# Loading the first slices of x in a gated GELU kernel: halves on two queues, and DMA transposes for slices 5 to 7

## The chip, the core and the metric

The kernel runs on one core of a Trainium2 chip. The metric is the time of one execution on the device in microseconds (us). Three executions of the kernel before took 592.37, 591.83 and 591.96 us; their median is 591.96 us. One more execution was profiled, and all rows shown below are from it.

## What is computed

x has 2048 rows of 1024, w_gate and w_up are 1024 by 3584, w_down is 3584 by 1024; everything is bfloat16.

```
g = jnp.einsum("bsd,df->bsf", x, w_gate)
u = jnp.einsum("bsd,df->bsf", x, w_up)
h = _gelu(g) * u            # tanh form
return jnp.einsum("bsf,fd->bsd", h, w_down)
```

## The kernel before, in words

The 2048 rows go in two halves of 1024, and each half in two chunks of 512 rows (`SCH`). TensorE needs x with the 1024 columns on the partitions, so a chunk is kept transposed as eight tiles `xT[c][ko]`, 128 by 512 each. "Slice ko" below means the 128 columns of x (or the 128 rows of a weight) that belong to `ko`. The 3584 hidden columns are 28 blocks of 128 in eight groups of 3, 3, 3, 3, 4, 4, 4, 4. For each block and chunk, eight matmuls 128x512 (one for each slice, L103) give g and eight give u. ScalarE and VectorE make `hT` of them (class `Evac`, L113 to L139). After all eight groups of a half, L307 multiplies `hT` by `w_down`, and the result is stored.

The schedule is written by hand (`manual_schedule`, L168): each engine runs its instructions in the order of the code.

**How the kernel begins.** Nothing is in the chip's memory yet, and the first group (three blocks, first chunk) is computed in an order of its own, `first_group` (L251): for slice 0, then slice 1 and so on, six matmuls, three with w_gate and three with w_up, into six PSUM banks. So slice k of x, of w_gate and of w_up must be there when step ko=k starts, and each step is 6 matmuls.

Meanwhile TensorE runs `dummy` matmuls (L174) on a constant: six before the first transposes (L182), then one of 512 and one of 256 columns behind them (L255, L256).

Of the first chunk of x, slices 0 to 5 (`NTURN = 6`) are loaded as they lie (`xpart`, L185, into the tiles `xn`) and turned on TensorE (`turn`, L224): four 128x128 transposes into a PSUM bank (L231), which VectorE copies to `xT` (L237; for slice 0 in two halves, L240 and L241). `turn(0)` stands ahead of everything, `turn(1)` behind the fifth matmul of step ko=0, and each other `turn(ko + 1)` behind the second matmul of step ko. Slices 6 and 7 are DMA transposes (`xload`, L96), which need no work on TensorE.

The loads go out from two queues, SP (`S`) and ACT (`A`), in the order of L200 to L217: x slice 0 on SP and w_gate slice 0 on ACT first, then the others, and the two DMA transposes last on SP. On ACT, a load of the Sigmoid table (L180) and a Square of one column (L181, which reads `gate`, set by VectorE at L178) stand ahead of the DMAs. Behind the first group's loads SP issues the weights of groups 1 and 2 (L219, L220, 768 KB each) and eight DMA transposes for the second chunk (L222).

**Waits between DMAs.** The framework hands eight completion counters round over the DMAs of both queues, in the program's merged order. A DMA on a counter that is in use waits, on its queue, until the DMA eight places earlier has landed; everything behind it on that queue waits too. In the kernel before, x slices 2-3 and w_gate slice 2 go out without a wait. w_up slice 2 waits for x slice 0, w_gate slice 3 for w_gate slice 1, w_gate slices 4-5 for x slices 2-3, w_gate slices 6-7 for w_gate slice 2, the first DMA transpose for w_up slice 2, the second for x slices 4-5.

Of the kernel before, what the change touches and what calls it, by code (L numbers as in the profile page):

```python
# [14 lines left out]
def kernel(  # L15
# [11 lines left out]
    nc = tc.nc  # L27
    P = nc.NUM_PARTITIONS
    bf16 = mybir.dt.bfloat16
    f32 = mybir.dt.float32  # L30
    ACT = mybir.ActivationFunctionType
    ALU = mybir.AluOpType

    x2 = x.flatten_outer_dims()
    out2 = out.flatten_outer_dims()
    S, Dm = x2.shape
    Df = w_gate.shape[1]
    NKB = Dm // P
    NFB = Df // P
    SCH = 512  # L40
# [6 lines left out]
    GROUPS = [3, 3, 3, 3, 4, 4, 4, 4]  # L47
# [5 lines left out]
    NST = 4  # L53
    WDF = 4
    NWARM = 6
    NTURN = 6
    TPC = SCH // P

    pool = ctx.enter_context(tc.tile_pool(name="sb", bufs=1))
# [11 lines left out]
    st_ring = [pool.tile([P, DMW], bf16, name=f"st{r}") for r in range(NST)]  # L71
    warm = nc.const_aps.tensor(1.0, (P, SCH), bf16)
    ident = pool.tile([P, P], bf16, name="ident")
    xn = [pool.tile([P, TPC, 2 * P], bf16, name=f"xn{q}") for q in range(NTURN // 2)]
    banks = [psum.tile([P, 512], f32, name=f"bank{b}") for b in range(8)]

    nbank = 0
# [1 line left out]
    def bank():  # L79
        nonlocal nbank  # L80
        b = banks[nbank % 8]
        nbank += 1
        return b
# [12 lines left out]
    def xload(half, c, ko):  # L96
        s0 = half * HS + c * SCH
        nc.sync.dma_start_transpose(
            out=xT[c][ko], in_=x2[s0 : s0 + SCH, ko * P : (ko + 1) * P]
        )  # L100

    def mm1(ps, w, j, c, ko):
        nc.tensor.matmul(  # L103
            ps,
            lhsT=w[:, ko, j * P : (j + 1) * P],
            rhs=xT[c][ko],
            start=(ko == 0),
            stop=(ko == NKB - 1),
        )
# [57 lines left out]

    ctx.enter_context(tc.manual_schedule())  # L168

    gate = pool.tile([P, SCH], bf16, name="gate")  # L170
    gated = pool.tile([P, 1], f32, name="gated")

    def dummy(b, n=SCH):
        nc.tensor.matmul(b[:, :n], lhsT=warm[:, :P], rhs=warm[:, :n], start=True, stop=True)  # L174

    nc.vector.memset(gate, 0.0)  # L178
    make_identity(nc, ident)
    nc.scalar.preload_act_table(ACT.Sigmoid)  # L180
    nc.scalar.activation(gated, gate[:, :1], ACT.Square)  # L181
    for _ in range(NWARM):  # L182
        dummy(banks[5])

    def xpart(eng, ko, n):  # L185
        eng.dma_start(
            out=xn[ko // 2][:, :, (ko % 2) * P : (ko % 2 + n) * P],
            in_=x2[0:SCH, ko * P : (ko + n) * P].rearrange("(t p) d -> p t d", p=P),
        )

    def wpart(eng, ring, w, ko, n):
        eng.dma_start(
            out=ring[0][:, ko : ko + n, : GROUPS[0] * P],
            in_=w[ko * P : (ko + n) * P, : GROUPS[0] * P].rearrange("(ko ki) f -> ki ko f", ki=P),
        )


    S, A = nc.sync, nc.scalar
    G, U = (wg_ring, w_gate), (wu_ring, w_up)
    xpart(S, 0, 1)  # L200
    wpart(A, *G, 0, 1)
    wpart(S, *U, 0, 1)
    xpart(A, 1, 1)
    wpart(S, *G, 1, 1)
    wpart(A, *U, 1, 1)
    xpart(S, 2, 2)
    xpart(A, 4, 2)
    wpart(S, *G, 2, 1)
    wpart(S, *U, 2, 1)
    wpart(S, *G, 3, 1)  # L210
    wpart(A, *U, 3, 1)
    wpart(S, *G, 4, 2)
    wpart(A, *U, 4, 2)
    wpart(S, *G, 6, 2)
    wpart(A, *U, 6, 2)
    for ko in range(NTURN, NKB):
        xload(0, 0, ko)  # L217
    for n in (1, 2):
        wload(nc.sync, wg_ring, w_gate, n, n)  # L219
        wload(nc.sync, wu_ring, w_up, n, n)  # L220
# [3 lines left out]
    def turn(ko):  # L224


        tp = [banks[6 + ko % 2].bitcast(bf16)] * 2
        if ko == 0:
            tp = [banks[6].bitcast(bf16), banks[7].bitcast(bf16)]
        for t in range(TPC):  # L230
            nc.tensor.transpose(  # L231
                tp[t // (TPC // 2)][:, t * P : (t + 1) * P],
                xn[ko // 2][:, t, (ko % 2) * P : (ko % 2 + 1) * P],
                ident,
            )
        if ko:
            nc.vector.tensor_copy(out=xT[0][ko], in_=tp[0][:, :SCH])  # L237
        else:
            h = SCH // 2
            nc.vector.tensor_copy(out=xT[0][ko][:, :h], in_=tp[0][:, :h])  # L240
            nc.vector.tensor_copy(out=xT[0][ko][:, h:], in_=tp[1][:, h:SCH])  # L241
# [9 lines left out]
    def first_group():  # L251
        wg, wu = wg_ring[0], wu_ring[0]
        ps = [(bank(), bank()) for _ in range(GROUPS[0])]
        turn(0)
        dummy(banks[5])  # L255
        dummy(banks[5], SCH // 2)  # L256
        n0 = GROUPS[0]
        for ko in range(NKB):
            steps = [(b, j) for j in range(n0) for b in range(2)]
            if ko == 0:  # L260
                steps = [(b, j) for b in range(2) for j in range(n0)]
            for i, (b, j) in enumerate(steps):
                mm1(ps[j][b], (wg, wu)[b], j, 0, ko)
                if i == (4 if ko == 0 else 1) and ko + 1 < NTURN:
                    turn(ko + 1)
        e = [Evac(ps[j][0], ps[j][1], j, 0) for j in range(GROUPS[0])]
        e[0].square()
        e[1].square()
        e[0].cubic()
        e[0].sigmoid()  # L270
        e[1].cubic()
        e[2].square()
        e[0].gelu()
        e[0].product()
        e[1].sigmoid()
        e[2].cubic()
        e[1].gelu()
        e[1].product()
        e[2].sigmoid()
        e[2].gelu()  # L280
        e[2].product()
# [34 lines left out]
    for half in range(NHALF):  # L316
        base = half * NG
        if half == 0:
            first_group()
            group(1, [0], ahead=2)  # L320
            group(2, [0])
            for g in range(NG):
                group(g, [1] if g < NW else range(HSC))
                i = g - 1
                if 0 <= i < len(wd):
                    for q in range(i, len(wd) if g == NG - 1 else i + 1):
                        nc.sync.dma_start(
                            out=wd[q],
                            in_=w_down[q * WDF * P : (q + 1) * WDF * P, :].rearrange(
                                "(fo fi) d -> fi fo d", fi=P  # L330
                            ),
                        )
                prefetch(g + 3)
        else:
            for g in range(NG):
                group(base + g, range(HSC))
                prefetch(base + g + 3)
        k = 0
        xnext = [(c, ko) for c in range(HSC) for ko in range(NKB)] if half + 1 < NHALF else []
        for ss in range(HS // P):  # L340
            for dc in range(NDC):
# [8 lines left out]
                if xnext:  # L350
                    c, ko = xnext.pop(0)
# [31 lines left out]
```

## Time and profile before

| what | us |
|---|---|
| median of three executions | 591.96 |
| profiled execution, its own time | 591.85 |
| span of its profile, first to last instruction | 590.1 |
| around the span (591.85 - 590.1) | 1.75 |
| TensorE busy | 583.5 (99%) |
| dummies (L174), eight, busy | 3.6 |
| transposes on TensorE (L231), 24, busy | 2.6 |
| DMA transposes (L98), 26, median from issue to landing | 2.7 |

A row of the timeline reads: start in us from the beginning of the span, us, engine, line, operation, output<-input, shape, xcount, and in brackets the idle time before it with what ended it. SPq and ACTq rows are the issuing of a DMA by that queue. PEld is TensorE's weight load, PE its matmul. The us of a matmul is from its start to its modelled end; matmuls overlap, so what a matmul costs in a stream is read from one start to the next start. A row of the DMA view gives out<-in, the issuing queue, xcount, the size, and the us from issue to landing. A row of the chain of waits gives start, us, and the work that the end of the program waited for.

### The profile page before, as it was taken

How to read it: one execution, taken by the hardware profiler on the slowest of the kernel's cores; microseconds unless marked ns; L12 is line 12 of the kernel's file. 1: busy time of each engine (PE TensorE's matmuls, PEld its weight loads, DVE VectorE, ACT ScalarE, POOL GpSimd, SP SyncE). 2: the span in 40 equal slices, each digit the busy share in tenths (PEclk: the TensorE clock that was granted, in tenths of full speed). 3: DMA queues.
4: the chain of work that ended last, by engine and by line, in shares of the span. 5: the costliest groups of instructions: out<-in, count | busy, mean ns of one | idle time of the engine just before them, and what ended most of it. 6: DMA issues, size and time to landing. Idle time of an engine off the chain costs nothing.

```text
span 590.1 us, 6588 instructions
## 1 busy us (share of the span) xinstructions
PE 583.5 (99%) x2723; PEld 269.1 (46%) x2776; DVE 244.0 (41%) x361; ACT 147.7 (25%) x243; POOL 0.7 (0%) x6
## 2 busy tenths in 40 slices
PE   9999999999999999999999999999999999999998
PEld 4444444444444444444444444444444444444445
DVE  1765665565656400000046565566556562000000
ACT  1443333333333200000023333333333331000000
POOL 0000000000000000000000000000000000000000
PEclk9999999999999999999999999999999999999999
DMA  9905936055050311111203034214000000000000
GB/s 230 224 10 185 316 106 214 11 204 178 1 178 1 107 48 43 45 46 36 55 18 107 17 126 143 84 59 131 13 1 1 2 1 9 19 26 19 27 19 27
DMA packets 58317, 45.51 MB, mean 77 GB/s; under 512 B 16816, under 2 KB 54704, under 8 KB 58288
## 3 DMA queue, kind: packets, MB, share of 16 engines
q1 hardware_dynamic: 56256, 44.02, 24.7%
q10 hardware_dynamic: 2032, 1.08, 0.7%
q8 instruction: 21, 0.34, 0.2%
q14 instruction: 8, 0.07, 0.0%
HBM read 37.49 MB, written 4.19 MB: 71 GB/s over the span
## 4 chain that ended last, share of the span: by engine, by line
PE 99%; issue 0%; DVE 0%; ACT 0%
PE bank L103 65%; PE bank L307 33%; PE bank L174 1%; PE bank L231 0%; DVE xT L237 0%; ACT st L299 0%
## 5 line engine op out<-in xcount | busy, mean ns | idle before, releaser
L103 PE MATMUL bank<-xT,wg 128*128 128x512 bf16 x880 | 213.8, 380 | 1.2 <-DVE xT L237 0.3
L103 PE MATMUL bank<-xT,wu 128*128 128x512 bf16 x876 | 213.1, 379 | 1.0
L307 PE MATMUL bank<-wd,hT 128*128 128x512 bf16 (+2 forms) x935 | 193.0, 366 | 0.9
L307 PEld LDWEIGHTS <-hT 128*128 128x128 bf16 x952 | 90.9, 98 | 103.0
L103 PEld LDWEIGHTS <-wu 128*128 128x128 bf16 x896 | 87.8, 98 | 105.9 <-issue 1.1
L103 PEld LDWEIGHTS <-wg 128*128 128x128 bf16 x896 | 87.9, 98 | 105.4 <-issue 0.6
L125 ACT ACTIVATE sq<-bank 128x512 f32<-128x512 f32 x112 | 66.7, 596 | 172.7 <-PE bank L103 166.8
L136 DVE TENSOR_TENSOR tt<-sg,bank 128x512 bf16<-128x512 bf16 x112 | 77.0, 687 | 76.0 <-ACT sg L133 75.9
L128 DVE SCALAR_TENSOR_TENSOR wq<-sq,bank 128x512 f32<-128x512 f32 x112 | 76.8, 687 | 65.3 <-ACT sq L125 65.2
L133 ACT ACTIVATE sg<-wq 128x512 bf16<-128x512 f32 x112 | 70.5, 629 | 88.4 <-DVE wq L128 88.4
L301 DVE CAST st<-bank 128x512 bf16<-128x512 f32 (+2 forms) x17 | 11.1, 652 | 178.3 <-PE bank L307 166.9
L139 DVE TENSOR_TENSOR hT<-tt,bank 128x512 bf16<-128x512 bf16 x112 | 76.9, 687 | 12.4 <-DVE tt L136 0.9
L299 ACT CAST st<-bank 128x512 bf16<-128x512 f32 (+1 forms) x17 | 9.7, 568 | 178.1 <-PE bank L307 178.1
L237 DVE COPY xT<-bank 128x512 bf16<-128x512 bf16 x5 | 2.1, 424 | 6.8 <-PE bank L231 6.8
L174 PE MATMUL bank<-const-bfloat16-1.0 128*128 128x512 bf16 (+1 forms) x8 | 3.6, 601 | 0.8 <-PEq L367 0.8
L231 PEld LDWEIGHTS <-xn 128*128 128x128 bf16 x24 | 2.0, 107 | 2.0 <-DMA xn<-in_x_dram 0.6
L231 PE MATMUL bank<-ident,xn 128*128 128x128 bf16 x24 | 2.6, 235 | 0.0
L174 PEld LDWEIGHTS <-const-bfloat16-1.0 128*128 128x128 bf16 x8 | 1.0, 140 | 1.8 <-issue 1.8
L180 ACT ACT_TABLE_LOAD x1 | 1.3, 1283 | 0.7 <-PEq L367 0.7
L240 DVE COPY xT<-bank 128x256 bf16<-128x256 bf16 x1 | 0.3, 292 | 2.6 <-PE bank L231 2.6
L178 DVE MEMSET gate<- 128x256 uint32 x1 | 0.3, 272 | 0.9 <-PEq L367 0.9
masks.py:199 POOL TENSOR_SCALAR_AFFINE_SELECT ident<-ident 128x128 bf16<-128x128 bf16 x1 | 0.3, 293 | 0.1
(7 smaller groups left out, 1.1 us busy)
## 6 DMA issues: line engine op xcount, KB each, us to landing
wg<-in_w_gate_dram SPq DMA_DIRECT2D x8, 1024.0 KB, 5.3
wu<-in_w_up_dram SPq DMA_DIRECT2D x8, 1024.0 KB, 7.3
wd<-in_w_down_dram SPq DMA_DIRECT2D x7, 1024.0 KB, 8.8
wg<-in_w_gate_dram SPq DMA_DIRECT2D x7, 768.0 KB, 4.7
wu<-in_w_up_dram SPq DMA_DIRECT2D x7, 768.0 KB, 6.3
out_dram<-st SPq DMA_DIRECT2D x31, 128.0 KB, 1.7
xT<-in_x_dram SPq DMA_TRANSPOSE x26, 2.7
wu<-in_w_up_dram ACTq DMA_DIRECT2D x2, 192.0 KB, 4.0
```

Of the source, the lines that this page charges most:

```text
L103: nc.tensor.matmul(ps, lhsT=w[:, ko, j * P : (j + 1) * P], rhs=xT[c][ko], start=(ko == 0), stop=(ko == NKB - 1),)
L125: nc.scalar.activation(self.sq, self.g, ACT.Square, scale=GELU_SQRT_C)
L128: nc.vector.scalar_tensor_tensor(out=self.wq, in0=self.sq, scalar=1.0, in1=self.g, op0=ALU.add, op1=ALU.mult)
L133: nc.scalar.activation(self.sg, self.wq, ACT.Sigmoid, scale=GELU_K)
L136: nc.vector.tensor_tensor(out=self.tt, in0=self.sg, in1=self.g, op=ALU.mult)
L139: nc.vector.tensor_tensor(out=self.dst, in0=self.tt, in1=self.u, op=ALU.mult)
L174: nc.tensor.matmul(b[:, :n], lhsT=warm[:, :P], rhs=warm[:, :n], start=True, stop=True)
L231: nc.tensor.transpose(tp[t // (TPC // 2)][:, t * P : (t + 1) * P], xn[ko // 2][:, t, (ko % 2) * P : (ko % 2 + 1) * P], ident,)
L237: nc.vector.tensor_copy(out=xT[0][ko], in_=tp[0][:, :SCH])
L299: nc.scalar.copy(out=st[:, :cw], in_=ps[:, :cw])
L301: nc.vector.tensor_copy(out=st[:, :cw], in_=ps[:, :cw])
L307: nc.tensor.matmul(ps[:, :cw], lhsT=hT[f][:, ss * P : (ss + 1) * P], rhs=wd[f // WDF][:, f % WDF, c0 : c0 + cw], start=(f == 0), stop=(f = ...
```

## The change

- x slice 0 goes as two halves, token blocks 0-1 on SP and 2-3 on ACT, each the first DMA of its queue.
- w_gate slice 0 goes as two halves of 64 partitions, the second DMA of each queue.
- `NTURN` is 5: slice 5 of x is a DMA transpose like 6 and 7 and has no `turn`. Slice 4 is a load of its own.
- The order of the first group's loads on the two queues is new: w_gate slice 2 and w_gate slices 6-7 move from SP to ACT, and the three DMA transposes stand on SP between.
- The table load moves behind ACT's DMAs; the Square of one column and the memset of `gate` are gone.
- One dummy of 512 columns ahead of the transposes has 128 columns; the one of 256 behind them has 128.
- `turn(1)` stands behind the fourth matmul of step ko=0, not the fifth.

With the new order the counters fall otherwise: x slices 2-3 wait for the ACT half of x slice 0, w_gate slice 2 for the SP half; w_up slices 2 and 3 wait for the halves of w_gate slice 0; w_gate slice 3 waits for x slice 1, x slice 4 for w_up slice 0, w_gate slices 4-5 for w_gate slice 1, w_up slices 4-5 for w_up slice 1. The DMA transposes of slices 5, 6 and 7 wait for x slices 2-3, w_up slice 2 and w_gate slice 3; w_gate slices 6-7 wait for w_gate slice 2, w_up slices 6-7 for w_up slice 3. The first weight of group 1 waits for x slice 4.

```
-    NTURN = 6
+    NTURN = 5
...
-    nc.vector.memset(gate, 0.0)
     make_identity(nc, ident)
-    nc.scalar.preload_act_table(ACT.Sigmoid)
-    nc.scalar.activation(gated, gate[:, :1], ACT.Square)
-    for _ in range(NWARM):
+    for _ in range(NWARM - 1):
         dummy(banks[5])
+    dummy(banks[5], P)
 
-    def xpart(eng, ko, n):
+    def xpart(eng, ko, n, t0=0, t1=TPC):
         eng.dma_start(
-            out=xn[ko // 2][:, :, (ko % 2) * P : (ko % 2 + n) * P],
-            in_=x2[0:SCH, ko * P : (ko + n) * P].rearrange("(t p) d -> p t d", p=P),
+            out=xn[ko // 2][:, t0:t1, (ko % 2) * P : (ko % 2 + n) * P],
+            in_=x2[t0 * P : t1 * P, ko * P : (ko + n) * P].rearrange("(t p) d -> p t d", p=P),
         )
...
-    xpart(S, 0, 1)
-    wpart(A, *G, 0, 1)
+    xpart(S, 0, 1, 0, TPC // 2)
+    xpart(A, 0, 1, TPC // 2, TPC)
+    wpart(S, *G, 0, 1, 0, P // 2)
+    wpart(A, *G, 0, 1, P // 2, P)
     wpart(S, *U, 0, 1)
     xpart(A, 1, 1)
     wpart(S, *G, 1, 1)
     wpart(A, *U, 1, 1)
     xpart(S, 2, 2)
-    xpart(A, 4, 2)
-    wpart(S, *G, 2, 1)
+    wpart(A, *G, 2, 1)
     wpart(S, *U, 2, 1)
+    wpart(A, *U, 3, 1)
     wpart(S, *G, 3, 1)
-    wpart(A, *U, 3, 1)
+    xpart(A, 4, 1)
     wpart(S, *G, 4, 2)
     wpart(A, *U, 4, 2)
-    wpart(S, *G, 6, 2)
+    xload(0, 0, 5)
+    wpart(A, *G, 6, 2)
+    xload(0, 0, 6)
     wpart(A, *U, 6, 2)
-    for ko in range(NTURN, NKB):
-        xload(0, 0, ko)
+    xload(0, 0, 7)
+    nc.scalar.preload_act_table(ACT.Sigmoid)
...
         dummy(banks[5])
-        dummy(banks[5], SCH // 2)
+        dummy(banks[5], P)
...
-                if i == (4 if ko == 0 else 1) and ko + 1 < NTURN:
+                if i == (3 if ko == 0 else 1) and ko + 1 < NTURN:
                     turn(ko + 1)
```

More of the change, by code (lines that the diff above doesn't have):

```diff
@@ L73 @@
     ident = pool.tile([P, P], bf16, name="ident")
-    xn = [pool.tile([P, TPC, 2 * P], bf16, name=f"xn{q}") for q in range(NTURN // 2)]
+    xn = [pool.tile([P, TPC, 2 * P], bf16, name=f"xn{q}") for q in range((NTURN + 1) // 2)]
     banks = [psum.tile([P, 512], f32, name=f"bank{b}") for b in range(8)]
@@ L168, with wpart @@
     ctx.enter_context(tc.manual_schedule())
-    gate = pool.tile([P, SCH], bf16, name="gate")
-    gated = pool.tile([P, 1], f32, name="gated")
     def dummy(b, n=SCH):
         nc.tensor.matmul(b[:, :n], lhsT=warm[:, :P], rhs=warm[:, :n], start=True, stop=True)
-    nc.vector.memset(gate, 0.0)
     make_identity(nc, ident)
-    nc.scalar.preload_act_table(ACT.Sigmoid)
-    nc.scalar.activation(gated, gate[:, :1], ACT.Square)
-    for _ in range(NWARM):
+    for _ in range(NWARM - 1):
         dummy(banks[5])
-    def xpart(eng, ko, n):
+    dummy(banks[5], P)
+    def xpart(eng, ko, n, t0=0, t1=TPC):
         eng.dma_start(
-            out=xn[ko // 2][:, :, (ko % 2) * P : (ko % 2 + n) * P],
-            in_=x2[0:SCH, ko * P : (ko + n) * P].rearrange("(t p) d -> p t d", p=P),
+            out=xn[ko // 2][:, t0:t1, (ko % 2) * P : (ko % 2 + n) * P],
+            in_=x2[t0 * P : t1 * P, ko * P : (ko + n) * P].rearrange("(t p) d -> p t d", p=P),
         )
-    def wpart(eng, ring, w, ko, n):
+    def wpart(eng, ring, w, ko, n, p0=0, p1=P):
         eng.dma_start(
-            out=ring[0][:, ko : ko + n, : GROUPS[0] * P],
-            in_=w[ko * P : (ko + n) * P, : GROUPS[0] * P].rearrange("(ko ki) f -> ki ko f", ki=P),
+            out=ring[0][p0:p1, ko : ko + n, : GROUPS[0] * P],
+            in_=w[ko * P : (ko + n) * P, : GROUPS[0] * P].rearrange("(ko ki) f -> ki ko f", ki=P)[
+                p0:p1
+            ],
         )
```

## The prediction

> **What bounds the kernel now.** I read the page's busy times first, then its chain of work that ended last.
>
> ```profile
> PE 583.5 (99%) x2723; PEld 269.1 (46%) x2776; DVE 244.0 (41%) x361; ACT 147.7 (25%) x243; POOL 0.7 (0%) x6
> ...
> PE 99%; issue 0%; DVE 0%; ACT 0%
> PE bank L103 65%; PE bank L307 33%; PE bank L174 1%; PE bank L231 0%; DVE xT L237 0%; ACT st L299 0%
> ```
>
> TensorE is the bound from end to end, so the time falls only where TensorE has work that isn't needed, waits, or runs slowly. The change touches the loads and order of the first group alone. So next the chain of waits in the first 18 us (start, us, what):
>
> ```profile
> 0.77 2.72 PE bank L174 x6
> 3.49 0.43 PE bank L231 x4
> 3.92 0.64 PE bank L174 x2
> 4.56 2.00 PE bank L103 x5
> 6.56 0.24 PE bank L231 x4
> 6.80 0.02 issue
> 6.82 0.43 DVE xT L237
> 7.25 0.04 issue
> 7.30 0.59 PE bank L103 x2
> ```
>
> Before 7.30 us there are eight dummies (L174), the transposes of slices 0 and 1 (L231), and one true wait: VectorE copies slice 1 while TensorE has nothing left of step ko=0. From there the chain is matmuls, with four transposes (0.22 us) in each of the steps ko=1 to 4. Then the timeline:
>
> ```profile
> 3.21 0.45 PEld L231 LDWEIGHTS <-xn 128*128 128x128 bf16 x4 [0.62 <-DMA xn<-in_x_dram]
> ...
> 6.62 0.38 PE L103 MATMUL bank<-xT,wu 128*128 128x512 bf16 x1
> ...
> 7.30 0.38 PE L103 MATMUL bank<-xT,wg 128*128 128x512 bf16 x1 [0.30 <-DVE xT L237]
> ...
> 7.82 2.50 SPq L98 DMA_TRANSPOSE xT<-in_x_dram  x2
> ```
>
> Slice 0 of x lands at 0.74 + 2.4 = about 3.15, its weight load starts at 3.21, and the first transpose at 3.28, which is also where the sixth dummy lets go. So dummies and data are in balance here, and shorter dummies pay only if the data come sooner.
>
> One more reading: 512 columns take 0.43 us from start to start in this stretch (4.35 to 5.63, three matmuls) and 0.215 us later (7.30, 7.51). The spacing halves at about 6.3 us. The granted-clock column reads 1.00 throughout, so I go by the spacing. Work taken out before 6.3 us is thus worth half its length at the end: the slow stretch doesn't get shorter, real matmuls move into it.
>
> **The change step by step.**
>
> *Start.* Five dummies end at 2.86 (the start of the sixth before); the 128-column one adds a quarter of 0.43, so TensorE is free at 2.97. When does x slice 0 land? No row shows a 64 KB half. On the side of a gain nothing in the trace lands sooner than the 128 KB stores (median 1.7 us), which would give 2.45, before TensorE is free; on the other side x slice 1 (128 KB, ACT) took 4.0, which would give 4.7. The nearest rows are the other first loads: 96 KB took 2.4 and 2.6, 128 KB took 2.4. Size hardly shows, so I take 2.3 us: landed at 3.04, and with the 0.12 us from landing to transpose seen above, the first transpose at 3.16, 0.12 us earlier. TensorE then waits 0.19 us where it ran a dummy.
>
> The ACT half goes out at 0.74 and not at 1.17 as ACT's first DMA did, since the table load (0.73) is out of its way. The w_gate halves go out at about 1.2, as the whole did; by the whole's 2.4 us to landing that is 3.6, ahead of the first real matmul.
>
> The Trainium skill ("DMA: Bandwidth & Descriptors", Rules for kernel authors) speaks against halves: two transfers to disjoint partition halves share the same 16 engines and gain nothing. Here w_gate is cut by partitions, and x by tokens, which changes nothing in that reason. By the rule the first transpose stays at 3.28, and the whole gain below comes to about 0.46 us in place of 0.52.
>
> *From transposes to the first matmul.* Before it was 4.35 - 3.28 = 1.07 us: four transposes at 0.107, then dummies of 0.43 and 0.21. Now the dummies are 0.43 and 0.11, 0.96 us in all; VectorE's second copy ends at 3.96 + 0.29 = 4.25, that is 0.97 behind the first transpose, and its signal takes about 0.05, so it binds at 1.02. First real matmul at 4.18.
>
> *turn(1) one matmul earlier.* Four matmuls at 0.43 end at 5.89. x slice 1 must be there: it landed at 1.62 + 4.0 = 5.6, and is issued at the same time as before. Four transposes at 0.107 to 6.31, the last starts at 6.21. Before, VectorE started 0.26 us after the last transpose's start (6.56 to 6.82); in the slow stretch a transpose is modelled 0.09 us longer (314 against 219 ns), so 6.55 here. Copy 0.43, signal 0.04: step ko=1 starts at about 7.0, before 7.30. **Gain 0.30 us.** The last two matmuls of ko=0 end at 6.74, so a wait of 0.26 us is left where 0.46 was.
>
> *turn(5) goes.* Four transposes, 12.28 to 12.50: **0.22 us**, all on the path, at full speed. VectorE's copy beside it was hidden.
>
> *Hidden edits.* The memset (0.27, VectorE idle till 3.74) and the Square of one column (0.20) were beside the dummies. The table load (1.28) now follows ACT's DMAs; these ended at 6.54 before and get two issues more, say 9, and ScalarE first works at 16.37. Without that cover the load would delay the first evacuation by at most 1.28.
>
> *The loads.* The new waits stand on SP: x slices 2-3 wait for half of slice 0 and go out at about 3.1 in place of 2.25; behind them queue w_up 2, w_gate 3, w_gate 4-5, the three transposes and all weights of the next groups. Before they landed at 2.25 + 4.6 = 6.85, behind w_gate slice 1 on their queue, which didn't land before 5.4; so a later issue is hidden in part and I put the landing between 6.85 and 7.7. Needed: step ko=1 at 7.0 plus two matmuls, 7.43. I take 6.9; the far end costs 0.3.
>
> The first DMA transpose waits for x slices 2-3: issue at about 6.95, then 1.25 each (2.50 for two), so 6.95, 8.2, 9.45. These rows give the time to land:
>
> ```profile
> xT<-in_x_dram SPq DMA_TRANSPOSE x1, 4.6
> ...
> xT<-in_x_dram SPq DMA_TRANSPOSE x1, 3.9
> ...
> xT<-in_x_dram SPq DMA_TRANSPOSE x1, 9.0
> ```
>
> The first is slice 6 before (7.82 to 12.4), the second the next one (landed at 13.0); the third went out behind four loads of 768 KB, which don't stand ahead here. With 4.6, 4.6 and 4.0 the slices land at 11.6, 12.8 and 13.5. Steps run 1.51 us with transposes (7.30 to 8.81) and 1.295 without, so ko=5, 6, 7 start at 12.8, 14.1, 15.4 (before 13.37, 14.66, 15.96). Slack 1.2, 1.3 and 1.9 us. Cost nothing; by 9.0 it would be 3.1.
>
> Group 1's first weight goes out at 10.7, not 10.36, and landed at 10.36 + 5.2 = 15.55; needed at about 16.6. The next, 7.0 us behind 10.99, is needed 3.45 later. Cost nothing; at worst, the whole extra issue of 1.25 passed on, 0.2.
>
> *Sum.* 0.30 + 0.22 = 0.52 us. Against the profiled execution's own 591.85 (span 590.1 and 1.75 around it) that is 591.33; against the median of three, which is 0.11 higher, 591.44. I predict **591.4 us**.
>
> **Rivals.**
>
> *The early data don't come earlier* (the halves land at 3.15 or later, or x slice 1 or slices 2-3 come some tenths late). For it: the balance at 3.2 us, and more small issues ahead. Then little but turn(5) is left and a few tenths are paid: 591.6 to 591.9.
>
> *Slower: slice 5 comes late.* Its DMA transpose is the last link of x slice 0, x slices 2-3, transpose, and lands among weight loads. It decides once slice 5 lands behind 12.8 us; to eat the gain it must land at 13.3, 6.4 us after its issue. For: the row of 9.0. Against: 4.6 and 3.9 in the same stretch. Price one for one, at 9.0 us 3.1: 592.0 to 594.5.
>
> *The fast spacing begins later.* TensorE now has a gap of 0.19 us at 3 us. If its speed-up hangs on unbroken work, each us of delay costs 0.5. Nothing in this trace shows what it hangs on. The Trainium skill ("TensorE: Matmul & The Clock Gate", Part 1) says activity is judged in free-running windows of about 3.4 us; a window lost would cost an estimated 1.7 us. No run here shows that, but the three executions, 0.54 us apart, suggest that executions of one kernel differ by such a thing. By the 0.54 alone: 591.9 to 592.4.
>
> *Better than the sum:* data at 2.97 or sooner, first transpose then at 2.97, gain 0.30 + 0.19 + 0.22 = 0.71: 590.9 to 591.2.
>
> **Chances.** Forecast (591.2 to 591.6) 0.55, early data not earlier 0.17, slice 5 late 0.10, later speed-up 0.09, better 0.09. The range 590.9 to 592.3 leaves out most of the slice-5 case and a little at the bottom. A measurement of this kernel can tell about 0.2%, or 1.2 us; the whole change moves less unless a transfer stalls. Faster by more (below 590.8) 0.06, slower by more (above 593.1) 0.08, between 0.86.
>
> **What would show it.** In the profile after: the first transposes at 3.1 to 3.2, the first L103 matmul at about 4.2, step ko=1 at 7.0, no transposes past 11 us, and the first group's end 0.5 us sooner than 17.25. I am wrong if a matmul of L103 waits for the DMA of xT or wg between 12 and 17 us, or if the 0.43 us spacing goes on past 6.5 us.

## The result and the profile after

Over 22 executions of each kernel, the changed kernel has a median of 592.37 us (591.73 to 593.48) and the kernel before 591.95 us (591.11 to 592.37). The medians are 0.42 us apart, where 0.52 us less had been predicted. The ratio, which goes by the means (592.59 and 591.89), is 1.0012 [1.0007, 1.0018]: slower by about 0.1%. The two sets differ in shape as well. 14 executions of the changed kernel lie between 591.73 and 592.63; the other 8 lie between 592.96 and 593.48, above every execution of the kernel before. I call these eight the late executions. The other fourteen have a median of 592.20, 0.25 us above that of the kernel before.

The profiled execution of the changed kernel took 592.14 us, with a span of 590.3, so it is not one of the late ones. Busy times and chain of its page:

```profile
PE 583.2 (99%) x2719; PEld 268.5 (45%) x2772; DVE 243.4 (41%) x359; ACT 147.5 (25%) x242; POOL 0.7 (0%) x6
...
PE 98%; DMA 1%; issue 1%; ACTq 0%; DVE 0%; ACT 0%
PE bank L103 65%; PE bank L307 33%; DMA wg<-in_w_gate_dram 1%; PE bank L231 0%; ACTq L179 0%; DVE xT L237 0%; ACT st L299 0%
```

TensorE does 0.3 us less, as the change meant it to. But a DMA stands in the chain now, and none did before. The chain of waits shows where (start, us, what):

```profile
1.25 3.41 DMA wg<-in_w_gate_dram
4.66 0.05 issue
4.71 1.82 PE bank L103 x4
...
6.79 0.44 DVE xT L237
...
7.27 0.59 PE bank L103 x2
```

The dummies (0.77 to 4.56 before) have left the chain. In their place stands one transfer, the ACT half of w_gate slice 0, issued at 1.25 and landed at 4.66. The first real matmul starts at 4.71, where it was 4.35 before. The timeline of TensorE shows this wait and a second one, at 13 us:

```profile
2.97 0.63 PE L231 MATMUL bank<-ident,xn 128*128 128x128 bf16 x4
...
4.71 1.46 PE L103 MATMUL bank<-xT,wg 128*128 128x512 bf16 x3 [0.57 <-DMA wg<-in_w_gate_dram]
...
13.02 0.38 PE L103 MATMUL bank<-xT,wu 128*128 128x512 bf16 x1
13.44 0.38 PE L103 MATMUL bank<-xT,wg 128*128 128x512 bf16 x1
```

At full spacing the matmul behind 13.02 would start at 13.23; it starts at 13.44. It is the first of step ko=5, and slice 5 landed at 13.40. The list of DMAs (KB, us from issue to landing) gives both transfers:

```profile
wg<-in_w_gate_dram ACTq DMA_DIRECT2D x1, 48.0 KB, 3.4
wg<-in_w_gate_dram SPq DMA_DIRECT2D x1, 48.0 KB, 2.6
...
xT<-in_x_dram SPq DMA_TRANSPOSE x1, 5.6
```

The first two rows are the halves; the whole slice took 2.4. The third is slice 5, issued at 7.78. Steps, before and after, read from the timelines:

```
                                    before    after   predicted
first transpose                      3.28      2.97     3.16
first real matmul                    4.35      4.71     4.18
step ko=1                            7.30      7.27     7.0
step ko=2                            8.81      8.91
step ko=5                           13.37     13.44    12.8
first matmul of group 1             17.25     17.32    16.7
end of the span (page)             590.1     590.3
```

So the profiled execution gains 0.31 us at the first transpose, gives 0.67 back at the first matmul, and gains again at step ko=1, because turn(1) stands one matmul earlier. It loses 0.13 at ko=2, where turn(2) waits for x slices 2-3 (landed 7.76), gains 0.22 by turn(5), and loses 0.21 to slice 5. The sum is 0.07 us later at the end of the first group. From there on the two kernels run in step: from the first matmul of group 1 to the start of the last matmul it is 569.88 us in both profiles.

**The end.** Another 0.22 us comes behind the last matmul. There SP's queue waits for the DMA counters (L378), two to an instruction, in a fixed order:

```profile
SPq L378 <- DMA out_dram<-st: 1.0, 1, 1.0
```

is the row of the kernel before, and of the changed one:

```profile
SPq L378 <- DMA out_dram<-st: 1.2, 1, 1.2
```

The last store landed 1.44 us after its issue before and 1.50 after. In the kernel before its counter stands in the third pair, so that two more instructions of 0.06 us follow the landing. The changed kernel issues 116 DMAs in place of 113 (a half more of x, a half more of w_gate, slice 5), which moves the last store on by three counters. Its counter now stands in the first pair, and all the rest follow: landing to the end of the waits takes 0.34 us, not 0.19. Together that makes 0.06 + 0.15 of the 0.22. It goes with the count of DMAs in all 19 profiles of this case, whatever else a kernel has changed: from the start of the last matmul to the end of the span it is 2.92 to 2.94 us with 113 DMAs, 2.98 to 3.01 with 114, 3.06 to 3.08 with 115 and 3.13 to 3.15 with 116.

### The profile page after: what moved, and what is told of

The parts are those of the page before. It is cut to its first block, busy times and chain, and to the rows that moved or that the text cites. A ratio compares the mean times of both kernels' runs of the same rounds, so it can differ in the third digit from the quotient of the medians.

```text
span 590.3 us, 6581 instructions
## 1 busy us (share of the span) xinstructions
PE 583.2 (99%) x2719; PEld 268.5 (45%) x2772; DVE 243.4 (41%) x359; ACT 147.5 (25%) x242; POOL 0.7 (0%) x6
## 3 DMA queue, kind: packets, MB, share of 16 engines
q10 hardware_dynamic: 2656, 1.26, 0.9%
## 4 chain that ended last, share of the span: by engine, by line
PE 98%; DMA 1%; issue 1%; ACTq 0%; DVE 0%; ACT 0%
PE bank L103 65%; PE bank L307 33%; DMA wg<-in_w_gate_dram 1%; PE bank L231 0%; ACTq L179 0%; DVE xT L237 0%; ACT st L299 0%
## 5 line engine op out<-in xcount | busy, mean ns | idle before, releaser
L103 PE MATMUL bank<-xT,wg 128*128 128x512 bf16 x880 | 213.8, 380 | 1.6 <-DMA wg<-in_w_gate_dram 0.6
L103 PE MATMUL bank<-xT,wu 128*128 128x512 bf16 x876 | 212.9, 379 | 1.0
L103 PEld LDWEIGHTS <-wg 128*128 128x128 bf16 x896 | 87.7, 98 | 106.4 <-DMA wg<-in_w_gate_dram 1.2
L103 PEld LDWEIGHTS <-wu 128*128 128x128 bf16 x896 | 87.7, 98 | 105.7 <-issue 0.7
```

The lines of the kernel that those rows point to most:

```text
L103: nc.tensor.matmul(ps, lhsT=w[:, ko, j * P : (j + 1) * P], rhs=xT[c][ko], start=(ko == 0), stop=(ko == NKB - 1),)
```

## The experiments

**Theories.** The expectations name them by number. *Theory 1, the cut:* halving w_gate slice 0 by partitions makes its landing later, and TensorE idles ahead of the first matmul. *Theory 2, slice 5:* its DMA transpose lands at 13.4 us and sets step ko=5, whatever comes earlier. *Theory 3, the load stream:* the three DMA transposes hold SP and the loads of the first group as a whole run about 1 us behind (by 14 us 2.77 MB have moved, 3.14 before: 198 and 224 GB/s), so slice 5, x slices 2-3 and group 1's first weight become late in turn, and undoing any one of them passes the wait on; issuing that weight on ACT would mend it. *Theory 4, the clock:* the idle time delays the halving of the matmul spacing, and that makes the late executions. Medians of the kernel before, run beside each, stand in brackets. In the diffs, `...` marks left-out lines.

**w_gate slice 0 whole again**, all else as changed.

```
-    wpart(S, *G, 0, 1, 0, P // 2)
-    wpart(A, *G, 0, 1, P // 2, P)
+    wpart(A, *G, 0, 1)
```

> The changed kernel with w_gate slice 0 again as one DMA of 96 KB on ACT, behind ACT's half of x slice 0. Theory 1 (the cut of w_gate slice 0 cost the gain): the first L103 matmul starts at 4.0 to 4.2 us in place of 4.71, step ko=1 at 6.8 to 7.0 in place of 7.27, and the median falls by 0.3 to 0.5 below the kernel before, to 591.4 to 591.7. Theory 2 (slice 5 by DMA transpose lands at 13.4 us and sets step ko=5, whatever comes earlier): the start comes earlier just the same, but step ko=5 stays at 13.4 and the median stays at 592.1 to 592.5, with some executions near 593.2.

Measured: 592.07 [591.57], ratio 1.0011 [1.0003, 1.002]. In its profile w_gate lands at 4.10, the first matmul starts at 4.15 and slice 5 is in time for ko=5. But group 1's first weight goes out at 11.36 and lands at 17.26:

```profile
17.30 1.04 PE L103 MATMUL bank<-xT,wg 128*128 128x512 bf16 x4 [0.28 <-DMA wg<-in_w_gate_dram]
```

The 0.4 us won at the start is lost at 17 us: the wait was passed on, to a place that neither theory 1 nor theory 2 had. Three of 11 executions lie at 593.08 to 593.59 although this kernel has no long wait ahead of its first matmul; no profile caught one.

**Slice 5 by turn(5) again**, all else as changed.

```
-    NTURN = 5
+    NTURN = 6
...
-    xpart(A, 4, 1)
+    xpart(A, 4, 2)
...
-    xload(0, 0, 5)
```

> The changed kernel with slice 5 turned on TensorE as before (x slices 4-5 as one load on ACT, no DMA transpose of slice 5); the halves stay. Theory 1: the first L103 matmul stays at 4.7, four transposes come back, step ko=5 at 13.4 to 13.5; the median is that of the changed kernel, 592.0 to 592.4, and its executions near 593.2 stay. Theory 2: the executions near 593.2 come from slice 5 landing later still; they go, all executions lie within 0.6 us, and the median is 592.0 to 592.2.

Measured: 592.01 [591.57], 1.0012 [1.0003, 1.002]. The half of w_gate lands at 4.68, and group 1's first weight, though issued 1.8 us sooner (9.79), lands only at 17.2. So it is not SP's queue alone that makes it late. Two of the 11 executions lie at 593.17 and 593.34: the late executions stay without a DMA transpose of slice 5, and theory 2 is wrong about them.

**Both undone**: the two diffs together.

> Both undone: w_gate slice 0 whole on ACT, slice 5 turned on TensorE; the x halves, the shorter dummies, the earlier turn(1) and the new order of the weights stay. Both theories together: first matmul at 4.0 to 4.2, step ko=1 at 6.8 to 7.0, no wait for slice 5, median 591.4 to 591.7, no execution above 592.2. Theory 1 alone says the same as for the whole w_gate slice alone, less 0.2 us of gain. If it is not below the kernel before, the order of the weights or the halves of x cost something too.

Measured: 591.56 [591.57], 1.0002 [0.9993, 1.001], no execution above 592.42. With both, the loss is gone, but no gain appears, though the halves of x, the shorter dummies and the earlier turn(1) are all in it. The first matmul starts at 3.98, and then x slice 1 (landed 5.87) and x slices 2-3 (7.44) are waited for.

**Only slice 5 by DMA, in the kernel before.**

```
-    NTURN = 6
+    NTURN = 5
...
-    xpart(A, 4, 2)
+    xpart(A, 4, 1)
```

> The kernel before with one part of the change alone: slice 5 as a DMA transpose ahead of those of slices 6 and 7 on SP, x slice 4 a load of its own on ACT. The prediction's working: four transposes (0.22 us) go from TensorE, slice 5 lands at about 12.4 and is needed at 13.15, median 591.7. Theory 2: three DMA transposes in a row among the weight loads land together at about 13.4 or later, step ko=5 waits 0.2 to 1.2 us, median 592.0 to 593.0.

Measured: 591.76 [591.57], 1.0004 [0.9995, 1.0013]. Here the transpose of slice 5 goes out at 7.49 and is quick:

```profile
xT<-in_x_dram SPq DMA_TRANSPOSE x1, 3.8
```

It lands at 11.32, with no wait, and step ko=4 takes 1.29 us in the profile where it took 1.52. The median shows no gain. In this kernel all of ACT's loads had landed by 9.8; in the changed one w_gate slices 6-7 and w_up slices 6-7 go out on ACT at 7.68 and 8.09 and land at 11.6 and 13.2, and the same transpose takes 5.6. That the loads beside it make it slow is the likeliest reading, and no run shows it alone.

**Group 1's first weight on ACT**, in the changed kernel.

```
+    wload(nc.scalar, wg_ring, w_gate, 1, 1)
...
-        wload(nc.sync, wg_ring, w_gate, n, n)
+        if n > 1:
+            wload(nc.sync, wg_ring, w_gate, n, n)
```

> The changed kernel with one edit: group 1's first weight (w_gate, 768 KB) is issued on ACT behind its last first-group load, not on SP behind the three DMA transposes. Theory 3 (each DMA transpose holds SP for 1.25 us and gives the DMA engines 128 KB, so the load stream falls about 1 us behind, and group 1's first weight, last in line, lands at 16.5 to 17.3 us when the first group has ended): the weight goes out at 8.6 us, lands before 15.8, no wait at the start of group 1, the executions near 593.2 go, and the median falls to 0.0 to 0.3 above the kernel before. Theory 1 (the cut w_gate slice 0 alone): nothing changes, 0.4 to 0.5 above before.

Measured: 593.77 [591.76], 1.0042 [1.003, 1.0054]. The weight goes out at 10.42 and not 8.6, because it waits for its counter, lands at 16.8, and slice 7's transpose beside it takes 6.8 us (lands 16.99): step ko=7 waits 1.2 us. SP's queue was not the remedy; the transfers are in each other's way.

**The start edits alone, in the kernel before**: x slice 0 in halves, shorter dummies, turn(1) earlier, table load later, Square and memset gone; w_gate whole, loads and turn(5) as before.

```
-    for _ in range(NWARM):
+    for _ in range(NWARM - 1):
         dummy(banks[5])
+    dummy(banks[5], P)
...
-    xpart(S, 0, 1)
+    xpart(S, 0, 1, 0, TPC // 2)
+    xpart(A, 0, 1, TPC // 2, TPC)
...
-                if i == (4 if ko == 0 else 1) and ko + 1 < NTURN:
+                if i == (3 if ko == 0 else 1) and ko + 1 < NTURN:
```

> The kernel before with the start edits alone: x slice 0 in halves on both queues, the short dummies, turn(1) behind the fourth matmul, the table load behind ACT's loads. w_gate slice 0 is whole, the order of the other loads and the turned slice 5 are those of before. The prediction's working for these steps gives 0.3 us less than before; theory 3 has them free, since the order of the loads behind stays: first matmul at 4.0 to 4.1, step ko=1 at 6.9, group 1's first weight at about 15.6, median 0.2 to 0.4 below before. If the halves of x alone take bytes out of flight, the median is that of before.

Measured: 591.99 [591.76], 1.0006 [0.9998, 1.0015]. First matmul at 4.02, ko=1 at 6.71, so the gain is made; and then it is lost at x slices 2-3, which land at 7.76 (6.86 before):

```profile
7.80 0.40 PE L229 MATMUL bank<-ident,xn 128*128 128x128 bf16 x4 [0.50 <-DMA xn<-in_x_dram]
```

One more DMA moves every later one to another counter, and x slices 4-5 went out 0.8 us sooner on ACT, against x slices 2-3.

**These with slice 5 by DMA and group 1's weight on ACT**: the changed kernel with w_gate slice 0 whole, the loads in the order of before, and the diff of the run on ACT.

> The start edits on the kernel before, slice 5 as a DMA transpose, and group 1's first weight on ACT: a version that theory 3 says keeps the whole gain. Expected 0.4 to 0.6 below before: first matmul at 4.0 to 4.1, no transposes of slice 5 on TensorE, slice 5 by 12.5, group 1 without a wait. If the weight of 768 KB among the DMA transposes delays these (slice 5 lands behind 12.8), the gain is eaten and the median is 0 to 1 us above before.

Measured: 594.81 [591.76], 1.0058 [1.0035, 1.0081]. The weight, 768 KB, goes out at 7.83, slice 5's transpose at 8.39, and the transpose takes 7.2 us:

```profile
15.66 0.58 PE L103 MATMUL bank<-xT,wg 128*128 128x512 bf16 x1 [2.91 <-DMA xT<-in_x_dram]
```

The profiled execution has a second price. Busy time by stretches (start, end, length; PE, PEld, DVE, ACT, POOL; granted clock, DMA share, GB/s):

```profile
12.80:15.60 2.80, 0.00 (x0) 0.00 (x0) 0.00 (x0) 0.00 (x0) 0.00 (x0) 0.93 1.43 97
15.60:18.60 3.00, 2.94 (x8) 0.99 (x8) 0.00 (x0) 0.00 (x0) 0.00 (x0) 0.50 1.13 309
18.60:22.00 3.40, 3.40 (x17) 1.57 (x16) 1.27 (x2) 1.64 (x4) 0.00 (x0) 1.00 1.10 327
```

After 2.9 us without work TensorE runs at half the clock from 15.66 to 18.6 us (8 matmuls in 3.0 us, where the same stretch of the kernel before has 16), so the wait costs about 1.5 us more than its length. And from 12.8 to 15.6 us, while the transposes are under way, the DMA engines are busy but move 97 GB/s.

**Slices 5 to 7 filled with zeros**, in the changed kernel; the three transposes are left out.

```
-    xload(0, 0, 5)
...
-    xload(0, 0, 6)
...
-    xload(0, 0, 7)
+    for ko in (5, 6, 7):
+        nc.gpsimd.memset(xT[0][ko], 0.0)
```

> The changed kernel without the three DMA transposes: slices 5 to 7 of the first chunk are set to zero by GpSimd, so that part of x is left out. Theory 3: SP issues group 1's first weight at about 8 us, it lands before 14.5, steps ko=5 to 7 and group 1 wait for nothing, and the median is 0.2 to 0.6 below the kernel before although the first matmul still starts at 4.7. Theory 1: the late start stays and with it the time of the changed kernel less the 0.2 us wait for slice 5, 0.1 to 0.3 above before.

Measured: 592.74 [591.76], 1.0015 [1.0006, 1.0023]: five executions at 591.62 to 592.13 and six at 592.74 to 593.49. The first profile, 591.62 us, has no wait behind the one for turn(2), and by 14 us 3.22 MB have moved (230 GB/s). So the transposes do thin out the stream; but their absence doesn't remove the late executions. That makes this kernel a good place to catch one.

**The same kernel, profiled twice more.**

> The changed kernel with slices 5 to 7 of the first chunk set to zero (no DMA transposes, that part of x is left out), one more profile. If its time is above 592.5: theory 4 has the spacing of 0.43 us going on past 7 us; theory 3 has a wait for w_gate slices 6-7 or for group 1's first weight, which had none in the first profile.

> The same kernel with slices 5 to 7 set to zero and the same reading: above 592.5, theory 4 has a spacing of 0.43 us past 7 us, theory 3 a wait for a load behind step ko=5.

Measured: 593.17 and 593.19, both late. The start of TensorE's timeline in the first of the two:

```profile
3.39 0.74 PE L171 MATMUL bank<-const-bfloat16-1.0 128*128 128x512 bf16 x2
5.19 1.44 PE L103 MATMUL bank<-xT,wg 128*128 128x512 bf16 x3 [1.06 <-DMA wg<-in_w_gate_dram]
...
8.13 0.63 PE L103 MATMUL bank<-xT,wg 128*128 128x512 bf16 x1
8.56 0.63 PE L103 MATMUL bank<-xT,wu 128*128 128x512 bf16 x1
...
9.41 0.44 PE L103 MATMUL bank<-xT,wg 128*128 128x512 bf16 x1
9.69 0.38 PE L103 MATMUL bank<-xT,wu 128*128 128x512 bf16 x1
```

and in the quick one of the same kernel:

```profile
4.66 1.22 PE L103 MATMUL bank<-xT,wg 128*128 128x512 bf16 x3 [0.48 <-DMA wg<-in_w_gate_dram]
5.71 0.38 PE L103 MATMUL bank<-xT,wu 128*128 128x512 bf16 x1
...
8.14 0.38 PE L103 MATMUL bank<-xT,wu 128*128 128x512 bf16 x1
8.35 0.38 PE L103 MATMUL bank<-xT,wg 128*128 128x512 bf16 x1
```

In the late one the matmuls still start 0.43 us apart at 8.13 and 8.56; the spacing halves at 9.5 us (9.75 in the other), and in the quick one at 5.5. Neither late one has a wait for a load behind the first matmul, as theory 3 would need. The halves of w_gate took 3.5 and 3.8 us to land (3.3 and 3.6 in the other), and TensorE idled for 1.06 us ahead of the first matmul (0.89 in the other). Four us more of half speed would cost up to 2; the difference measured is 1.55.

**The idle time filled**: the changed kernel with two more dummies of 512 columns ahead of the first real matmul.

```
         dummy(banks[5])
         dummy(banks[5], P)
+        dummy(banks[5])
+        dummy(banks[5])
```

> The changed kernel with two more dummies of 512 columns ahead of the first real matmul, so that TensorE does not stand idle from 3.9 to 4.7 us while the second half of w_gate slice 0 is on its way. Theory 4 (the executions near 593.2, 8 of 22, are those in which that idle time delays the halving of the matmul spacing): they go; all executions below 592.8 and the median at or below that of the changed kernel (0.0 to 0.4 above before) although the first real matmul starts no earlier. Theory 3 (the load stream): the late executions stay, median 0.4 to 0.6 above before.

Measured: 592.19 [591.83], 1.0008 [1.0, 1.0017]; all 11 executions at or below 592.59. Its first matmul starts at 5.02, later than in any profile of the changed kernel, and yet the late executions are gone. Were 8 in 22 the true share, none in 11 would come by luck with a chance of (14/22)^11, below 0.01; but that share is itself from few executions, and that all eight of these 33 fall among the 22 of the changed kernel has a chance of 0.023. The rest of the loss stays: in the profile TensorE still waits 0.50 us for slice 5.

**The kernel before without the two dummies behind the transposes.**

```
-        dummy(banks[5])
-        dummy(banks[5], SCH // 2)
```

> The kernel before without the two dummies behind the first transposes, so that TensorE stands idle from 3.7 to 4.3 us; no load changes and the first real matmul starts at 4.3 as before. Theory 4: some executions come out 0.8 to 1.7 us above the rest, at 592.7 to 593.5, which the kernel before has not. Theory 3 and the prediction's working: no difference, or 0.03 us less.

Measured: 591.39 [591.83], 0.9997 [0.9988, 1.0006], no late execution. I had expected some. The idle time that its profile shows ahead of the first matmul (4.30) is only 0.38 us, and the spacing halves at 4.4. The two late profiles above had 0.89 and 1.06 by the same reading; the profiles of the changed kernel had up to 0.68 and were not late. So in the profiles at hand the late ones are those with 0.89 us and more; whether the length alone decides is not shown. Later in the same profile TensorE waits 1.09 us for x slice 1, at 6.68, and the matmuls behind it keep the short spacing: a wait of this length behind the halving cost its length alone.

**turn(1) earlier alone, in the kernel before.**

```
-        dummy(banks[5], SCH // 2)
+        dummy(banks[5], P)
...
-                if i == (4 if ko == 0 else 1) and ko + 1 < NTURN:
+                if i == (3 if ko == 0 else 1) and ko + 1 < NTURN:
```

> The kernel before with no load touched: turn(1) behind the fourth matmul and the last dummy 128 columns. The prediction's working for these steps: first real matmul at 4.30, step ko=1 at 7.07 in place of 7.30, x slices 2-3 at 6.9 soon enough for turn(2) at 7.5; median 0.2 below before. If the load stream binds from slice 2 on, turn(2) waits and the median is that of before.

Measured: 591.41 [591.83], 0.9997 [0.9988, 1.0006]. Step ko=1 starts at 6.78 (7.30 before, 7.07 expected), no load is touched and nothing else waits. By the 7.07, some 0.3 of these 0.5 us is luck: in this execution the spacing halves at 5.8 us, in that of the kernel before at 6.3. The profiled execution is 0.5 us shorter than that of before (591.32), but the interval holds no change as well. It is the best candidate here, and no proven gain.

**The changed kernel, three more profiles**, to see how its early landings vary.

> The changed kernel once more, for a second profile. If it falls among the executions near 593.2, theory 4 has the matmul spacing at 0.43 us for longer than 6.5 us, theory 3 has slice 5 or group 1's first weight landing later than 14 or 17 us. If near 592.2, it shows how far the landing of the w_gate halves, of slice 5 and of group 1's weight move between executions.

> The changed kernel, one more profile. If its time is above 592.8: theory 4 has the spacing of 0.43 us going on past 7 us, theory 3 has it halved by 6.4 us and a landing later than in the profiles near 592.1 (slice 5 behind 14, group 1's first weight behind 17 us).

> The same kernel and the same reading as the third profile: above 592.8, theory 4 has a spacing of 0.43 us past 7 us, theory 3 a late landing.

Measured: 592.13, 592.36 and 592.29. In the four profiles slice 5 lands at 13.4 to 13.6 each time, so its wait is the rule. The first matmul starts at 4.71, 4.43, 4.11 and 4.82, as the later half of w_gate lands between 4.07 and 4.68. But step ko=5 starts at 13.44 to 13.60 in all four: where no execution is late, slice 5 decides, and an earlier first matmul gains nothing. None was a late execution. In the third the spacing halves only at 6.76, and group 1's weight lands at 17.49.

**The cut alone, in the kernel before.**

```
...
-    wpart(A, *G, 0, 1)
+    wpart(S, *G, 0, 1, 0, P // 2)
+    wpart(A, *G, 0, 1, P // 2, P)
```

> The kernel before with w_gate slice 0 in two halves of 64 partitions, one on SP behind x slice 0 (whole), one on ACT; nothing else. If the cut alone makes it late: the later half lands at 4.2 to 5.0 us (whole: 3.5), the first L103 matmul starts up to 0.6 us later than 4.35 and DMA moves under 190 GB/s from 2.5 to 4.5 us (212 before); the median is 0.1 to 0.5 above before, and executions near 593.2 are seen where TensorE's idle time reaches 1 us. If it took the halves of x as well: lands by 3.8, first matmul at 4.35, median that of before.

Measured: 592.27 [591.71], 1.0013 [1.0003, 1.0022], with two of 11 executions at 592.93 and 593.08: this one part makes as large a loss as the whole change, though not by the same path. Its profile:

```profile
wg<-in_w_gate_dram ACTq DMA_DIRECT2D x1, 48.0 KB, 3.0
wg<-in_w_gate_dram SPq DMA_DIRECT2D x1, 48.0 KB, 3.1
```

and, on TensorE,

```profile
9.10 0.39 PE L103 MATMUL bank<-xT,wu 128*128 128x512 bf16 x1 [0.51 <-DMA wu<-in_w_up_dram]
```

The halves land at 4.14 and 4.41 (the whole at 3.53), but the dummies fill the time, and the first matmul starts at 4.45, only 0.10 later than before. The further DMA takes one of the eight counters, so x slices 2-3 go out at 3.16 and not 2.25, and what stands behind them on SP comes later: w_up slice 2 lands at 9.06, and TensorE waits 0.51 us for it. What the loads move between 2.5 and 4.5 us is seen in the view by stretches, of the kernel before,

```profile
2.50:4.50 2.00, 2.00 (x10) 1.04 (x9) 0.50 (x2) 0.00 (x0) 0.00 (x0) 1.00 0.90 212
```

of this one, with the cut alone,

```profile
2.50:4.50 2.00, 2.00 (x10) 0.82 (x9) 0.51 (x2) 0.00 (x0) 0.00 (x0) 1.00 0.82 200
```

and of the changed one:

```profile
2.50:4.50 2.00, 1.63 (x9) 0.77 (x7) 0.50 (x2) 0.00 (x0) 0.00 (x0) 1.00 0.77 141
```

The last column is GB/s. The expected fall below 190 for the cut alone did not come. Over all profiles it is 141 to 178 in the ten of kernels that have both cuts, of x slice 0 and of w_gate slice 0, and 197 to 246 in the other nine. So the slower stream goes with the two cuts together; why is open. A packet of w_gate slice 0 takes 36 ns at the median, whole or cut, but the mean is 36 to 40 ns where the slice goes whole and 44 to 111 ns in a half: a few packets are much slower.

## Why the prediction was wrong, point by point

The prediction failed at two landings that it took from rows of the old trace, at a term that it left out (the end), and at the price of a rival. Both signs of being wrong that it named were seen: a matmul of L103 waits for xT at 13.44, and in the third profile the 0.43 us spacing goes on to 6.76. That 592.37 lies in the ranges of two rivals, *slice 5 late* and *the fast spacing begins later*, is partly luck: both were at work, but at other prices, and the 0.22 us at the end is in neither.

- **The step that failed first**: "The w_gate halves go out at about 1.2, as the whole did; by the whole's 2.4 us to landing that is 3.6, ahead of the first real matmul." The issue was right (1.25). The time to landing was 2.6 and 3.4 us in this profile and 2.6 to 3.8 over all. I priced a half by the whole's row and asked only whether it would gain. It costs: the first matmul is at 4.71. The cut alone gives as large a loss as the whole change, but in its profile by a counter (w_up slice 2 goes out later, and TensorE waits 0.51 us for it) and hardly by the first matmul (0.10). The Trainium skill ("DMA: Bandwidth & Descriptors", Rules for kernel authors) advises against cutting by partitions because the halves share the same engines. I had quoted that against the gain and spent it on x, where the halves landed well (2.1 and 2.3 us); for w_gate the runs show more than no gain, a loss.
- **x in halves, first transpose**: right, and better than predicted (2.97, the time at which the dummies end). It bought nothing, since the first matmul waited for w_gate.
- **turn(1) earlier**: the mechanism is right. From first matmul to step ko=1 it takes 2.56 us, where it took 2.95 and 2.82 was predicted; in the kernel before alone ko=1 comes at 6.78, partly by an earlier halving of the spacing. The 0.30 us were used up by the late first matmul.
- **turn(5) goes, 0.22 us**: right, the transposes are gone from step ko=4, but the step "The first is slice 6 before ... With 4.6, 4.6 and 4.0 the slices land at 11.6, 12.8 and 13.5. ... Cost nothing" failed for slice 5: issued 0.8 us later than predicted (7.78) because x slices 2-3 landed at 7.76, and 5.6 us under way, it landed at 13.40. The change also moves weights onto ACT beside the transposes, and I took durations from a trace in which they didn't stand there. This is the mechanism of the rival *slice 5 late*, at a price of 0.21 us. In executions that are not late it is the step that counts: ko=5 was predicted at 12.8 and starts at 13.44 to 13.60 in all four profiles.
- **x slices 2-3**: the far end of the bound (7.7) came true, and cost 0.1 in the profiled execution.
- **Group 1's first weight, priced at nothing and at worst 0.2**: held in the profiled execution (landed 16.54), but the slack I counted as free is used up. It binds in the third profile of the changed kernel and in the run with w_gate whole, where an earlier wait is taken away.
- **The hidden edits**: right. The table load waits 8.6 us for ACT's DMAs and delays nothing.
- **Not in the sum at all**: the end of the kernel. Three DMAs more shift the last store's counter, and that costs 0.22 us with the landing, over 500 us after the change.
- **The rival of the speed-up**: I gave it a price of 0.54 from the spread of before. The eight late executions lie 0.8 to 1.3 us above the median of the other fourteen, and in the variant with zeros the price is 1.55. The Trainium skill ("TensorE: Matmul & The Clock Gate", Part 1) speaks of free-running windows of about 3.4 us. The half clock after the long wait, from 15.2 to 18.6 us, agrees with it. So do the halvings without a long wait ahead of the first matmul, which lie between 4.25 and 6.76 us over the profiles, and the two late ones: 9.54 and 9.75 less 3.4 is 6.1 and 6.3, inside that range, as if one window had not counted as busy. The prediction counted the idle time at 0.19 us; it became 0.57 in this profile.

So the loss has three terms. By the means it is 0.69 us: the fourteen executions that are not late lie 0.30 above the kernel before, and the eight late ones add 0.39. Of the 0.30 the end is 0.22, in all four profiles of the changed kernel, and that is shown. The first group gains nothing (0.07 lost in the profiled execution), because each gain is taken by the next late transfer; that is shown by the runs in which one or both of the edits are undone. For the late executions, shown are the mechanism in the variant with zeros, and that they vanish when the idle time is filled. That the changed kernel's own eight have the same cause is inferred, since no profile of it caught one. Open are the three late executions with w_gate whole, for which I have no cause, and how the loss divides in the kernel in which the cut stands alone: its two late executions and the 0.51 us wait for w_up were not separated; the end, with 114 DMAs, makes about 0.07 of it.

## What to carry to other kernels

Where a start is balanced between dummies and data, the loads behind it follow one another closely: an edit that wants one transfer sooner must be priced by which next transfer becomes late, and slack found in the old trace is not free once several edits draw on it. Count DMAs, not only bytes: in this kernel each one more takes a counter, moves the waits of later DMAs, and shifts even the end. Price a cut transfer by a row of a cut transfer, and keep TensorE occupied until the first real data are sure to be there, because here a wait of about 1 us ahead of the first matmul cost that much again in clock.

## What the hardware showed unexpectedly

- 48 KB to 64 partitions took 2.6 to 3.8 us to land, and the same slice whole, 96 KB to 128 partitions, 2.3 to 3.0 over the runs.
- A DMA transpose of 128 x 512 in the first group held SP for 1.19 to 1.26 us. It landed in 3.8 us where ACT's loads had all landed by 9.8, in 5.6 to 6.3 beside the 192 KB weight loads on ACT of the changed kernel, and in 6.8 to 7.2 beside a load of 768 KB.
- The granted-clock column reads 1.00 in the first microseconds while the spacing of the matmuls is still 0.43 us. The spacing is the safer sign there.
- With 2.9 us without work in mid-kernel the clock was granted at half from about 15.2 to 18.6 us, for 3.4 us. A wait of 1.09 us at 6.7, in another run, left the spacing short.
- The DMAs of this kernel are waited for at its end two counters at a time: 113 DMAs left 2.92 to 2.94 us behind the start of the last matmul, 116 left 3.13 to 3.15.
